# RWKV attention, tanh FFN and top-1 experts: logits and third block's first tile reordered, and one run of matmuls per tile from the fourth block on

## The chip, the cores and the metric

The kernel runs on one core of a Trainium2 chip. A core has a matrix engine (PE; its weight loads are shown apart as PEld), a vector engine (DVE), a scalar engine (ACT), a general engine (POOL) and an engine that here issues transfers (SP). The engines run side by side and wait for each other through semaphores. The metric is the device time of one execution in microseconds (us); lower is better.

## The reference

Four sequences of 768 tokens, eight heads of 48 numbers. Three stages follow each other:

```
for t in range(S):                                  # linear attention with a decaying state
    cur = einsum('bhd,bhe->bhde', u * k_t, v_t)
    y_t = einsum('bhd,bhde->bhe', r_t, state + cur)
    state = w * state + einsum('bhd,bhe->bhde', k_t, v_t)
h = x @ w_in; x = (h - tanh(h)) @ w_out             # 3072 tokens, 384 -> 2048 -> 384
expert_idx = argmax(normalize(x) @ normalize(expert_emb).T / tau)
out = gate * (relu(x @ w1[e]) @ w2[e])              # the one expert e that the token chose
```

Everything is float32.

## The kernel before, in words

The 3072 tokens are 24 tiles of 128, three tiles to a block, so eight blocks (0 to 7); a sequence is six tiles. The recurrence is done tile by tile: with the decay multiplied into r and k, the products of a tile's tokens among each other (*scores*, line 407) are masked and, with a diagonal for the bonus u, multiplied by v, and the state of the tile before is added (*values*, line 438); `state_product` (line 458) and `state_add` (469) carry the state on. The last tile of a sequence has no state product, the first no state part in values. On PE the three differ in shape: scores contract over 48 rows, the two head groups side by side; values write 32 columns each, four turns side by side; the state product writes 48 columns.

The FFN runs over a block of 384 tokens and over 16 slices of 128 of its 2048 inner columns. A *step* is one slice: `ffn1` (line 534, nine matmuls, for float32 is split into a high and a low part) into a PSUM bank ph, tanh and a split on ACT and DVE (lines 581 to 611), then `ffn2` (line 545, nine matmuls) into three banks acc that stay open over the block. ffn2 comes some steps after its ffn1. After its 16 steps a block is finished: normalized, logits by expert, choice, place counts (`finish`, PE lines 646 to 656). After all blocks the eight experts run over the tokens gathered by expert; that part is not touched.

The program is in three parts. A start, written out by hand for the attention of tiles 0 to 2 and the first slices. Then 22 hand-ordered steps: 6 of block 0 and the 16 of block 1, during which the FFN weights are converted into their parts (`convert_next`, `split`, DVE lines 253 to 259 and ACT line 266), and tiles 3 to 5 are done. The output weights also yield logits columns: class `Logits` has `turn` (transposes, line 282, and their copies wt, 284), `product` (291, lt 294) and `back` (298, 300), one per step in turn. Here the transposed k (`turned`, line 352) is copied to ktok by ACT (`turned_rows`, line 357), and the diagonal am is made by ACT in eight pieces (line 393). Then a loop over the blocks 0, 2, 3 ... 7: block j's steps, with the attention of the next block woven in by the generator `attention`, advanced by a counter, 18 pieces in 12 steps (8 for the rest of block 0). Each tile there is: decays, diagonal and ktok on DVE and POOL, scores, a few pieces later values and state product and results.

Within the engines' queues the instructions keep the order in which a scheduler puts them; it mostly follows the written order, may shift an instruction that it holds to be late, and is bound by `tc.issue_after`. PE takes its queue strictly in order. `fence` holds a tile's first instructions behind a given other one. `fill` (line 525) puts spare matmuls of ones into a bank that is written anew afterwards; NWARM (line 154) counts such matmuls at the very start.

Of the kernel before, what the change touches and what calls it, by code (L numbers as in the profile page):

```python
# [9 lines left out]
F32R = mybir.dt.float32r  # L10
# [3 lines left out]
AF = mybir.ActivationFunctionType  # L14
# [15 lines left out]
def rwkv__then__tanh_ffn__then__top1_moe_kernel(  # L30
# [14 lines left out]
    nc = tc.nc  # L45
# [32 lines left out]
    COL0 = (13, 15)  # L78
    NATT = 12
    NATT0 = 8  # L80
    ICOL = 6
    NWARM = 13
    ISTORE = 14
# [245 lines left out]
    class Att:  # L329
# [56 lines left out]

        def diagonal(self, on_act=False):
            self.am = []
            for g in range(2):
                a = work.tile([P, HP, P], F32, name="am", bufs=4)  # L390
                if on_act:
                    for q in range(HP):
                        nc.scalar.activation(out=a[:, q, :], in_=ident, func=AF.Copy, scale=self.cd[:, q, g:g + 1])
                else:
                    nc.gpsimd.tensor_tensor(out=a, in0=ident[:, None, :].to_broadcast([P, HP, P]),  # L395
                                            in1=self.cd[:, :, g:g + 1].to_broadcast([P, HP, P]), op=ALU.mult)
                self.am.append(a)
# [31 lines left out]
        def values(self, part=0, of=1, idle=0):  # L429
# [6 lines left out]
            for turn in self.todo[part * n // of:(part + 1) * n // of]:  # L436
                for g, (kk, lhs, rhs, start, stop) in enumerate(turn):
                    nc.tensor.matmul(out=self.py[32 * g:32 * g + 32, kk, :], lhsT=lhs, rhs=rhs, start=start, stop=stop)

# [38 lines left out]

    def attn_tile(n, xt):
        t = Att(n, xt)  # L480
        with ExitStack() as es:
# [13 lines left out]
        yield  # L495

        t.values()
        t.state()
# [15 lines left out]
    def attention(j):  # L514
        xts[j] = work.tile([P, NK, 2, TOK], F32R, name="xt")
        for n in range(TB * j, TB * j + TB):
            if 2 * TB + 1 < n + 1 < NTILE:
                load_rkv(n + 1)
            yield from attn_tile(n, xts[j])

# [665 lines left out]
    a[0].decay_k(nc.vector)  # L1186
    a[0].scores(range(HP), 5)
    a[0].turned()
# [63 lines left out]
    def attention_stage(i):  # L1252

        later = []
        for n, first in zip(range(TB, 2 * TB), START):
# [6 lines left out]
            if i == first + 1:  # L1262
# [3 lines left out]
                t.turned()  # L1266
                t.diagonal(DACT)
                t.turned_rows()
            elif i == first + 2:
# [22 lines left out]
    def step2(j, i, g):  # L1292
        if i == spans[j][0]:
            accs[j] = [ps.tile([P, DL], F32, tag="p", name=f"acc{t}") for t in range(TB)]
        ffn2(i, spans[j], g, wout, accs[j])

    steps = [(0, f) for f in range(FA)] + [(1, f) for f in range(NF)]
    spans[0] = (0, FA)
# [3 lines left out]
    for i in range(len(steps) + 1):  # L1302
# [33 lines left out]
        for f in later:  # L1336
            f()
        if i in turns:
            c = turns[i]
            logits.append(Logits(c, ready[2 * c + 1][0]))  # L1340
            logits[c].turn()
            done.add(2 * c + 1)
        if i - 2 in turns:
            logits[turns[i - 2]].back()
        if i - 1 in turns:
            logits[turns[i - 1]].product()
        if m < NF:
# [3 lines left out]
        if i == 9:  # L1351
            fence[2 * TB] = mark["glo"], last[1]
        load_next()
# [4 lines left out]
        if i == ISTORE:  # L1358
            store_x(1, xts[1])
    del xts[1]  # L1360

# [16 lines left out]
    for j in (0, *range(2, NB)):  # L1378
        xt = xts.pop(j)
        store_x(j, xt)  # L1380
        att = attention(max(j + 1, 2)) if j + 1 < NB else iter(())
        na = 0
        natt = NATT if j > 0 else NATT0
        for n, i in enumerate(range(*spans[j])):
            ph = ffn1([win(p, i) for p in range(2)], columns_of(xt), NK, TOK)
            pend.append((j, i, small_tanh(ph, squares(ph), j * NF + i)))
            while na < (n + 1) * 18 // natt:
                next(att, None)
                na += 1
            if len(pend) > LAG:  # L1390
                ffn2_next()
# [13 lines left out]
            if j == NB - 1 and i in COL0:  # L1405
                next(wides[0])
        for _ in att:
            pass
    while pend:
# [81 lines left out]
```

## Time and profile before

| | us |
|---|---|
| median of 3 runs | 800.43 (799.94 to 801.45) |
| profiled execution | 802.88 |
| its span, first to last instruction | 801.3 |
| PE busy | 772.8 (96%) |
| DVE busy | 506.8 (63%) |
| ACT busy | 451.5 (56%) |
| POOL busy | 283.9 (35%) |

The profile shows one execution. Its busy times are per engine, and its timeline lists instructions in order of time with neighbours of one kind merged; a row's duration is from the first start to the last end of the merged instructions. Since matmuls are pipelined, the distance from one row's start to the next row's start tells more than the durations. An idle time stands in brackets with what ended it.

### The profile page before, as it was taken

How to read it: one execution, taken by the hardware profiler on the slowest of the kernel's cores; microseconds unless marked ns; L12 is line 12 of the kernel's file. 1: busy time of each engine (PE TensorE's matmuls, PEld its weight loads, DVE VectorE, ACT ScalarE, POOL GpSimd, SP SyncE). 2: the span in 40 equal slices, each digit the busy share in tenths (PEclk: the TensorE clock that was granted, in tenths of full speed). 3: DMA queues.
4: the chain of work that ended last, by engine and by line, in shares of the span. 5: the costliest groups of instructions: out<-in, count | busy, mean ns of one | idle time of the engine just before them, and what ended most of it. 6: DMA issues, size and time to landing. Idle time of an engine off the chain costs nothing. (4 is left out here: it accounts for less than half of the span.)

```text
span 801.3 us, 15575 instructions
## 1 busy us (share of the span) xinstructions
PE 772.8 (96%) x5938; PEld 726.3 (91%) x5938; DVE 506.8 (63%) x1080; ACT 451.5 (56%) x1044; POOL 283.9 (35%) x296
## 2 busy tenths in 40 slices
PE   8889999999999999999999999999999999999992
PEld 5679898889999999999999999999989999999992
DVE  7977975677866865775875775766554445454410
ACT  5675776637456556556656666785443444444421
POOL 3721640383550740651651530143340412332111
PEclk9899999999999999999999999999999999999997
DMA  8834350233330240231222201160653534554300
GB/s 277 285 94 135 113 184 14 86 86 121 90 134 21 70 135 38 87 93 80 86 69 105 86 2 60 31 187 31 193 150 112 167 115 155 181 176 146 106 28 31
DMA packets 41861, 87.33 MB, mean 109 GB/s; under 512 B 9744, under 2 KB 21440, under 8 KB 40754
## 3 DMA queue, kind: packets, MB, share of 16 engines
q1 hardware_dynamic: 37042, 76.74, 29.8%
q0 software_dynamic: 4320, 9.51, 3.6%
q8 instruction: 48, 0.79, 0.4%
q14 instruction: 35, 0.29, 0.2%
q10 hardware_dynamic: 416, 0.00, 0.0%
HBM read 67.46 MB, written 19.47 MB: 108 GB/s over the span
## 5 line engine op out<-in xcount | busy, mean ns | idle before, releaser
L534 PE MATMUL ph<-xt,wq 128*128 128x384 f32 (+2 forms) x1712 | 341.3, 342 | 2.5 <-ACT wt L284 1.4
L534 PEld LDWEIGHTS ph<-xt,wq 128*128 128x128 f32 x1712 | 302.7, 189 | 7.6 <-ACT wt L284 1.5
L545 PE MATMUL acc<-wq,ghi 128*128 128x392 f32 (+2 forms) x1120 | 289.9, 344 | 0.0
L545 PEld LDWEIGHTS acc<-wq,ghi 128*128 128x128 f32 (+1 forms) x1120 | 200.3, 187 | 5.4 <-issue 1.4
L545 PE MATMUL acc<-wq,glo 128*128 128x392 f32 (+2 forms) x560 | 185.2, 341 | 0.3 <-DVE glo L611 0.3
L581 ACT ACTIVATE z<-ph 128x384 f32<-128x384 f32 x128 | 62.6, 489 | 88.9 <-PE ph L534 88.7
L545 PEld LDWEIGHTS acc<-wq,glo 128*128 128x128 f32 (+1 forms) x560 | 104.0, 187 | 1.3 <-DVE glo L611 0.6
L592 ACT ACTIVATE ghi<-ph 128x384 fp32r<-128x384 f32 x128 | 62.7, 490 | 73.6 <-DVE ph L591 69.0
L590 DVE TENSOR_TENSOR ph<-ph,z 128x384 f32<-128x384 f32 x128 | 71.9, 561 | 46.3 <-ACT z L581 45.4
L597 DVE TENSOR_TENSOR glo<-ph,ghi 128x384 fp32r<-128x384 f32 x128 | 70.9, 554 | 40.1 <-ACT ghi L592 39.7
L778 POOL DMA_INDIRECT out_dram<-ob,gts x27 | 28.8, 1068 | 155.4 <-ACT ob L858 149.9
L582 ACT ACTIVATE q<-z,sb_t 128x384 f32<-128x384 f32 x128 | 79.0, 617 | 3.6
L591 DVE SCALAR_TENSOR_TENSOR ph<-q,ph 128x384 f32<-128x384 f32 x128 | 71.8, 561 | 12.5 <-ACT q L582 3.6
L611 DVE SCALAR_TENSOR_TENSOR glo<-ph,ghi 128x384 fp32r<-128x384 f32 (+2 forms) x56 | 31.6, 564 | 74.9 <-ACT ghi L610 66.7
L594 ACT ACTIVATE mk<-z,lz_t 128x384 bf16<-128x384 f32 x128 | 77.1, 602 | 0.0
L610 ACT ACTIVATE ghi<-ph 128x384 fp32r<-128x384 f32 (+2 forms) x56 | 27.8, 497 | 72.5 <-PE ph L534 66.6
L827 DVE TENSOR_TENSOR wq<-eraw,wq 128x768 fp32r<-128x768 f32 x60 | 55.1, 956 | 12.0 <-ACT wq L826 10.4
L826 ACT ACTIVATE wq<-eraw 128x768 fp32r<-128x768 f32 x64 | 50.5, 838 | 6.5 <-DMA eraw<-in_moe_w_dram 6.1
L267 POOL TENSOR_TENSOR wq<-wraw,wq 128x768 fp32r<-128x768 f32 (+1 forms) x17 | 31.0, 1823 | 61.9 <-ACT wq L266 61.9
L380 POOL TENSOR_TENSOR rk<-rkv 128x384 f32<-128x384 f32 x18 | 18.4, 1024 | 92.2 <-ACT xr L631 45.2
L395 POOL TENSOR_TENSOR am<-ident,cd 128x512 f32<-128x512 f32 x36 | 37.4, 1064 | 10.2 <-DVE cd L385 10.2
L346 POOL TENSOR_TENSOR tt<-tt,tab_k 112x512 f32<-112x512 f32 x20 | 33.1, 1657 | 17.8 <-DMA tt<-in_cols_dram 17.8
(282 smaller groups left out, 888.0 us busy)
## 6 DMA issues: line engine op xcount, KB each, us to landing
eraw<-in_moe_w_dram SPq DMA_DIRECT2D x32, 768.0 KB, 5.1
rkv<-in_rows_dram SPq DMA_DIRECT2D x18, 640.0 KB
tt<-in_cols_dram SPq DMA_DIRECT2D x22, 448.0 KB, 4.0
xd<-xt SPq DMA_DIRECT2D x8, 1152.0 KB, 8.4
wraw<-in_moe_w_in_dram SPq DMA_DIRECT2D x8, 768.0 KB
wraw<-in_moe_w_out_dram SPq DMA_DIRECT2D x8, 768.0 KB, 6.9
xs<-xr SPq DMA_DIRECT2D x21, 192.0 KB, 2.2
rkv<-in_rows_dram SPq DMA_DIRECT2D x4, 256.0 KB, 10.7
```

Source lines behind the costliest of these rows:

```text
L395: nc.gpsimd.tensor_tensor(out=a, in0=ident[:, None, :].to_broadcast([P, HP, P]), in1=self.cd[:, :, g:g + 1].to_broadcast([P, HP, P]), op=A ...
L534: mark["ph"] = nc.tensor.matmul(out=ph, lhsT=lhs[a][:, kk, :], rhs=rhs(b, kk), start=(kk == 0 and p == 0), stop=(kk == nk - 1 and p == 2)).ins
L545: mm = nc.tensor.matmul(out=acc[t], lhsT=g[a][:, t * P:t * P + m], rhs=rhs(b, i), start=(i == span[0] and p == 0), stop=(i == span[1] - 1 ...
L581: nc.scalar.activation(out=z, in_=ph, func=AF.Square)
L582: nc.scalar.activation(out=q, in_=z, func=AF.Square, scale=SS, bias=sb_t)
L590: nc.vector.tensor_tensor(out=ph, in0=ph, in1=z, op=ALU.mult)
L591: nc.vector.scalar_tensor_tensor(out=ph, in0=q, scalar=KC, in1=ph, op0=ALU.add, op1=ALU.mult)
L592: mark["ghi"] = nc.scalar.activation(out=ghi, in_=ph, func=AF.Copy).ins
L594: nc.scalar.activation(out=mk, in_=z, func=AF.Relu, bias=lz_t, accum_out=zx[:, step:step + 1])
L597: mark["glo"] = nc.vector.tensor_tensor(out=glo, in0=ph, in1=ghi.bitcast(F32), op=ALU.subtract).ins
L826: nc.scalar.activation(out=hi[c][:, a], in_=t[:, a], func=AF.Copy)
L827: engs[s % len(engs)].tensor_tensor(out=lo[c][:, a], in0=t[:, a], in1=hi[c][:, a].bitcast(F32), op=ALU.subtract)
```

## The change

- Start: 17 instead of 13 first matmuls of ones, 4 instead of 5 fills in the first scores.
- Steps of blocks 0 and 1: ktok is issued behind the first half of the diagonal; in a step, Logits' back and product are now written ahead of turn. The decay of tile 7 gets the fence that tile 6 has.
- The third block's attention (`third`) begins in the last four of the 22 steps and is advanced by another rule in the rest of block 0.
- From block 2 on (attention of tiles 9 to 23), the generator is replaced by `prepare(n)` (decays, diagonal, ktok) and `turn(n)`: values and state product of tile n-1, scores of tile n right behind them, and only then the results, the state's sum and the mask. `turn` stands at steps 0, 4, 8, 12 of block 2 and 2, 7, 12 of the later ones.

```diff
@@ -76,10 +76,8 @@
     NEARLY = 1
     NNAR = 2
     COL0 = (13, 15)
-    NATT = 12
-    NATT0 = 8
     ICOL = 6
-    NWARM = 13
+    NWARM = 17
     ISTORE = 14
     FA = 6
     START = (0, 1, 2)
@@ -384,13 +382,17 @@
             self.cd = work.tile([P, HP, 2], F32, name="cd")
             nc.vector.tensor_reduce(out=self.cd.rearrange("p a b -> p (a b)"), in_=self.rk, op=ALU.add, axis=AX.X)
 
-        def diagonal(self, on_act=False):
+        def diagonal(self, on_act=False, between=None):
             self.am = []
             for g in range(2):
                 a = work.tile([P, HP, P], F32, name="am", bufs=4)
                 if on_act:
                     for q in range(HP):
-                        nc.scalar.activation(out=a[:, q, :], in_=ident, func=AF.Copy, scale=self.cd[:, q, g:g + 1])
+                        ins = nc.scalar.activation(out=a[:, q, :], in_=ident, func=AF.Copy,
+                                                   scale=self.cd[:, q, g:g + 1]).ins
+                    if between and g == 0:
+                        with tc.issue_after(ins):
+                            between()
                 else:
                     nc.gpsimd.tensor_tensor(out=a, in0=ident[:, None, :].to_broadcast([P, HP, P]),
                                             in1=self.cd[:, :, g:g + 1].to_broadcast([P, HP, P]), op=ALU.mult)
@@ -435,7 +437,8 @@
             n = len(self.todo)
             for turn in self.todo[part * n // of:(part + 1) * n // of]:
                 for g, (kk, lhs, rhs, start, stop) in enumerate(turn):
-                    nc.tensor.matmul(out=self.py[32 * g:32 * g + 32, kk, :], lhsT=lhs, rhs=rhs, start=start, stop=stop)
+                    mark["py"] = nc.tensor.matmul(out=self.py[32 * g:32 * g + 32, kk, :], lhsT=lhs, rhs=rhs,
+                                                  start=start, stop=stop).ins
 
         def result_hi(self):
             tok = slice((self.n % TB) * P, (self.n % TB + 1) * P)
@@ -476,8 +479,8 @@
             self.state_product()
             self.state_add()
 
-    def attn_tile(n, xt):
-        t = Att(n, xt)
+    def attn_tile(n):
+        t = Att(n, None)
         with ExitStack() as es:
             for x in fence.pop(n, ()):
                 es.enter_context(tc.issue_after(x))
@@ -494,6 +497,10 @@
         yield
         yield
 
+        j = n // TB
+        if j not in xts:
+            xts[j] = work.tile([P, NK, 2, TOK], F32R, name="xt")
+        t.xt = xts[j]
         t.values()
         t.state()
         t.result()
@@ -512,11 +519,42 @@
                               in_=xt.rearrange("p k i t -> p (k i t)").bitcast(F32))
 
     def attention(j):
-        xts[j] = work.tile([P, NK, 2, TOK], F32R, name="xt")
         for n in range(TB * j, TB * j + TB):
             if 2 * TB + 1 < n + 1 < NTILE:
                 load_rkv(n + 1)
-            yield from attn_tile(n, xts[j])
+            yield from attn_tile(n)
+
+    running = {}
+
+    def prepare(n):
+        t = running[n] = Att(n, None)
+        t.decay_r(nc.vector)
+        t.decay_k(nc.gpsimd)
+        t.bonus(nc.gpsimd)
+        t.sums()
+        t.diagonal()
+        t.decayed()
+
+    def turn(n):
+
+        t = running.pop(n - 1, None)
+        if t:
+            j = (n - 1) // TB
+            if j not in xts:
+                xts[j] = work.tile([P, NK, 2, TOK], F32R, name="xt")
+            t.xt = xts[j]
+            t.values()
+            t.state_product()
+        if n in running:
+            with tc.issue_after(mark["py"]) if t else ExitStack():
+                running[n].scores(range(HP))
+        if t:
+            t.result()
+            t.state_add()
+        if n in running:
+            running[n].causal()
+        if t and n + 1 < NTILE:
+            load_rkv(n + 1)
 
 
     def fill(bank, n):
@@ -1184,7 +1222,7 @@
     a[0].summed()
     a[0].decay_r(nc.vector)
     a[0].decay_k(nc.vector)
-    a[0].scores(range(HP), 5)
+    a[0].scores(range(HP), 4)
     a[0].turned()
     a[0].diagonal(True)
     routing_constants()
@@ -1264,8 +1302,7 @@
                 t.summed()
                 t.scores(range(HP))
                 t.turned()
-                t.diagonal(DACT)
-                t.turned_rows()
+                t.diagonal(DACT, t.turned_rows)
             elif i == first + 2:
                 t.causal()
             elif i == first + 3:
@@ -1294,6 +1331,7 @@
             accs[j] = [ps.tile([P, DL], F32, tag="p", name=f"acc{t}") for t in range(TB)]
         ffn2(i, spans[j], g, wout, accs[j])
 
+    third = attention(2)
     steps = [(0, f) for f in range(FA)] + [(1, f) for f in range(NF)]
     spans[0] = (0, FA)
 
@@ -1335,21 +1373,21 @@
             pass
         for f in later:
             f()
+        if i - 2 in turns:
+            logits[turns[i - 2]].back()
+        if i - 1 in turns:
+            logits[turns[i - 1]].product()
         if i in turns:
             c = turns[i]
             logits.append(Logits(c, ready[2 * c + 1][0]))
             logits[c].turn()
             done.add(2 * c + 1)
-        if i - 2 in turns:
-            logits[turns[i - 2]].back()
-        if i - 1 in turns:
-            logits[turns[i - 1]].product()
         if m < NF:
             last = split(*ready[m])
             if m % 2 == 0:
                 done.add(m)
         if i == 9:
-            fence[2 * TB] = mark["glo"], last[1]
+            fence[2 * TB] = fence[2 * TB + 1] = mark["glo"], last[1]
         load_next()
         if i == 1:
             behind.close()
@@ -1357,6 +1395,9 @@
             decay_rows()
         if i == ISTORE:
             store_x(1, xts[1])
+
+        if len(steps) - 4 <= i < len(steps):
+            next(third)
     del xts[1]
 
 
@@ -1378,15 +1419,22 @@
     for j in (0, *range(2, NB)):
         xt = xts.pop(j)
         store_x(j, xt)
-        att = attention(max(j + 1, 2)) if j + 1 < NB else iter(())
-        na = 0
-        natt = NATT if j > 0 else NATT0
+        na = 4
+
+        at = () if j in (0, NB - 1) else (0, 4, 8, 12) if j == 2 else (2, 7, 12)
+        n0 = TB * (j + 1) + (j > 2)
         for n, i in enumerate(range(*spans[j])):
             ph = ffn1([win(p, i) for p in range(2)], columns_of(xt), NK, TOK)
             pend.append((j, i, small_tanh(ph, squares(ph), j * NF + i)))
-            while na < (n + 1) * 18 // natt:
-                next(att, None)
+            while j == 0 and na < 5 + 3 * n // 2:
+                next(third, None)
                 na += 1
+            if n - 1 in at and n0 + at.index(n - 1) + 1 < NTILE:
+                prepare(n0 + at.index(n - 1) + 1)
+            if j == 2 and n == 0:
+                prepare(n0)
+            if n in at:
+                turn(n0 + at.index(n))
             if len(pend) > LAG:
                 ffn2_next()
             if n >= LAG:
@@ -1404,8 +1452,10 @@
                 next(ld, None)
             if j == NB - 1 and i in COL0:
                 next(wides[0])
-        for _ in att:
-            pass
+        if j == 0:
+            for _ in third:
+                pass
+            load_rkv(3 * TB + 1)
     while pend:
         ffn2_next()
     for _ in fin:
```

On PE, at the first of the later tiles (block 2's steps), the order of before. `pa` are scores, `py` values, `pst` the state product, `acc` and `ph` the FFN:

```order
L407 MATMUL pa_2707<-tt 128x128
L545 MATMUL acc_2596<-wq_77,ghi 128x392
...
L438 MATMUL py<-am,rkv_118 32x128 x4
L458 MATMUL pst<-rkv_118,ktok 48x48 x8
L545 MATMUL acc_2595<-wq_78,ghi 128x392
L545 MATMUL acc_2595<-wq_81,ghi 128x392
```

And the order now, at a tile of the same block:

```order
L440 MATMUL py<-am,rkv_123 32x128 x4
L461 MATMUL pst<-rkv_123,ktok 48x48 x8
L409 MATMUL pa_3075<-tt 128x128
L409 MATMUL pa_3076<-tt 128x128
...
L583 MATMUL acc_2567<-wq_79,ghi 128x392
L583 MATMUL acc_2567<-wq_82,ghi 128x392
```

The scores have moved from a place of their own between ffn1 and ffn2 to the place behind the state product of the tile before. The order has 14 such runs, one for each of the tiles 10 to 23.

On PE, in the third block's attention (tile 8, with the rest of block 0's steps), before:

```order
L407 MATMUL pa_2232<-tt 128x128 x4
L545 MATMUL acc_2033<-wq_82,ghi 128x392
...
L407 MATMUL pa_2233<-tt 128x128 x4
L545 MATMUL acc_2034<-wq_79,glo 128x392
...
L438 MATMUL py<-tt,st_120 32x128 x4
L545 MATMUL acc_2032<-wq_79,ghi 128x392
```

And now, the same tile:

```order
L409 MATMUL pa_2235<-tt 128x128
L409 MATMUL pa_2236<-tt 128x128
...
L583 MATMUL acc_2035<-wq_79,ghi 128x392
...
L440 MATMUL py<-tt,st_124 32x128 x4
L440 MATMUL py<-am,rkv_122 32x128 x4
```

Before, the scores of the two head groups are apart, and values begin, stop for FFN matmuls and go on. In the order now the scores, values and state products of tiles 7 and 8 stand whole, between ffn1 and ffn2; the scores of tile 6 have the first three matmuls of one group ahead of the first three of the other.

On PE, at the start of step 3, before and now (`pt` turn, `pl` product, `ps_k` transposes of k):

```order
L352 MATMUL ps_k<-ident,tt 128x112 x4
L282 MATMUL pt<-ident,wraw 128x128 x6
L291 MATMUL pl<-wt,ent 32x128 x6
L525 LDWEIGHTS ones_93
L525 MATMUL ph<-ones_93 128x384
```

```order
L350 MATMUL ps_k<-ident,tt 128x112 x4
L289 MATMUL pl<-wt,ent 32x128 x6
L280 MATMUL pt<-ident,wraw 128x128 x6
L563 LDWEIGHTS ones_93
L563 MATMUL ph<-ones_93 128x384
```

The product has moved ahead of the transposes; the four fills and the step's ffn1 stay behind both.

## Rows read from the trace of the kernel before

**Rows 1.** The page: busy time, share of the span, instructions.
```profile
PE 772.8 (96%) x5938; PEld 726.3 (91%) x5938; DVE 506.8 (63%) x1080; ACT 451.5 (56%) x1044; POOL 283.9 (35%) x296
```

**Rows 2.** Waits of PE: who waited for whom, total us, times, longest.
```profile
PE pl L291 <- ACT ktok L357: 2.4, 1, 2.4
...
PE ph L534 <- ACT wt L284: 1.4, 1, 1.4
...
PE py L438 <- DVE am L412: 0.9, 1, 0.9
```

**Rows 3.** Timeline of PE, block 2's steps: start us, us, line, count.
```profile
221.03 1.73 PE L534 MATMUL ph<-xt,wq 128*128 128x384 f32 x9
222.68 1.16 PE L407 MATMUL pa<-tt 48*128 48x128 f32 x16
223.77 0.63 PE L545 MATMUL acc<-wq,ghi 128*128 128x392 f32 x2
...
225.50 1.74 PE L534 MATMUL ph<-xt,wq 128*128 128x384 f32 x9
227.07 0.52 PE L545 MATMUL acc<-wq,ghi 128*128 128x392 f32 x2
...
228.68 1.74 PE L534 MATMUL ph<-xt,wq 128*128 128x384 f32 x9
230.35 0.42 PE L438 MATMUL py<-tt,st 112*32 112x128 f32 x8
...
232.03 0.56 PE L458 MATMUL pst<-rkv,ktok 128*48 128x48 f32 x16
232.52 0.63 PE L545 MATMUL acc<-wq,ghi 128*128 128x392 f32 x2
...
234.25 1.74 PE L534 MATMUL ph<-xt,wq 128*128 128x384 f32 x9
```

**Rows 4.** Busy time of each engine from tile 6's scores to tile 9's.
```profile
140.33:189.62 49.29, 48.05 (x463) 42.84 (x462) 33.30 (x75) 27.61 (x67) 29.89 (x28) 1.00 0.35 105
```

**Rows 5.** PE by line in that stretch: count, busy us, mean ns, idle.
```profile
L534 PE MATMUL ph<-xt,wq 128*128 128x384 f32 x100 | 19.8, 341 | 0.3 <-ACT xr L631 0.3
L545 PE MATMUL acc<-wq,ghi 128*128 128x392 f32 x60 | 16.5, 350 | 0.0
L545 PE MATMUL acc<-wq,glo 128*128 128x392 f32 x30 | 10.5, 348 | 0.0
```

**Rows 6.** Timeline of PE, tile 8's scores.
```profile
168.58 1.16 PE L407 MATMUL pa<-tt 48*128 48x128 f32 x8
169.67 0.45 PE L545 MATMUL acc<-wq,ghi 128*128 128x392 f32 x1
...
170.58 1.16 PE L407 MATMUL pa<-tt 48*128 48x128 f32 x8
```

**Rows 7.** Timeline of PE, start of step 3.
```profile
45.27 0.85 PE L291 MATMUL pl<-wt,ent 128*32 128x128 f32 x12 [2.41 <-ACT ktok L357]
...
46.58 3.24 PE L534 MATMUL ph<-xt,wq 128*128 128x384 f32 x9
```

**Rows 8.** Timelines of ACT and of DVE, the same time.
```profile
44.74 0.48 ACT L357 ACTIVATE ktok<-ps_k 128x384 f32<-128x384 f32 x1
...
38.97 1.18 DVE L343 TENSOR_TENSOR tt<-tt,tab_r 112x512 f32<-112x512 f32 x1
...
45.12 0.73 DVE L412 COPY_PREDICATED am<-cmask,pa 128x512 f32<-128x512 uint8 x1
```

**Rows 9.** A stretch of 10 us: busy time of PE, PEld, DVE, ACT, POOL, then PEclk.
```profile
40.00:50.00 10.00, 7.59 (x63) 6.36 (x66) 7.75 (x17) 6.82 (x20) 3.47 (x2) 0.83 0.30 91
```

**Rows 10.** Timeline of ACT, the wait of 1.4 us in rows 2.
```profile
87.15 0.88 ACT L266 ACTIVATE wq<-wraw 128x768 fp32r<-128x768 f32 x1
```

**Rows 11.** Timeline of PE, the first matmuls.
```profile
1.70 4.74 PE L154 MATMUL warm<-ones 128*128 128x512 bf16 x12
7.02 1.05 PE L370 MATMUL ps_cd<-u_pair,rows 112*128 112x2 f32 x8 [0.58 <-DVE rows L364]
```

## The prediction, made before the change was run

> **What bounds the kernel now.** I read the page's engine shares first, then PE's waits, then PE's timeline. The reader is to see that PE is busy for 772.8 of 801.3 us, 96% [rows 1], and that its named waits are few: 2.4, 1.4 and 0.9 us are the largest that the change touches [rows 2]. So neither another engine nor a transfer sets the time; PE's own queue does, and a change can only win in two ways: take one of these short waits away, or make PE do the same matmuls in less time. The second needs starts, not durations, since neighbouring matmuls overlap: how far one group's start lies from the next group's start. The row groups of block 2 give this for every kind of neighbour [rows 3].
>
> The profiled execution took 802.88 us, 2.45 more than the median of 800.43. The sum below is made against 802.88 and then carried over to the median.
>
> **One run of values, state product and scores: 14 times.** From block 2's steps [rows 3]: an undisturbed ffn1 takes 227.07 - 225.50 = 1.57 us to the start of ffn2, an undisturbed ffn2 228.68 - 227.07 = 1.61. With scores between, ffn1 takes 222.68 - 221.03 = 1.65 (0.08 more), the scores 223.77 - 222.68 = 1.09, and the ffn2 behind them 225.50 - 223.77 = 1.73 (0.12 more). A scores group thus costs 1.29. Values and state product cost 0.10 on the ffn1 ahead (230.35 - 228.68 = 1.67), 232.03 - 230.35 = 1.68 and 232.52 - 232.03 = 0.49 of their own, and 0.12 on the ffn2 behind (234.25 - 232.52 = 1.73): 2.39. Apart, the two cost 3.68. Put in one run, one way in and one way out of the FFN's matmuls goes: 0.10 + 1.68 + 0.49 + 1.09 + 0.12 = 3.48. So 0.20 per run, and for 14 runs 2.8 us. The number of matmuls stays the same, so nothing more can come from here.
>
> What the trace of before never shows is scores right behind a state product. Bounds: 0.20 per run, if that neighbour costs no more than an FFN matmul there; nothing, if going from one shape to the other costs as much again as the exit and the entry saved, so 0 to 2.8 in all. I take the upper end: the state product took its 0.49 to the FFN, and the nearest change from one small shape to another, values to state product, shows no gap beyond the rows' own time [rows 3].
>
> What could be late next: the run's four banks (two of scores, one each of values and state product) with the three open acc leave one of the eight for ph. By the waits that the programs write, the next ffn1's bank is one that the FFN's own DVE work gives back, which is done about a step ahead. I put no wait there; the rival below prices one. prepare's decays and diagonal on POOL and DVE come one step after the run before; the next run is four or five steps later (steps of 3.18 us, so some 13 us) and DVE and POOL were busy 33.30 and 29.89 of 49.29 us when attention ran beside the FFN [rows 4]: covered. The loads, SP's DMAs, are issued after the run of the tile before and have as long; they are not behind anything new.
>
> **The third block's attention.** From tile 6's scores to tile 9's took 49.29 us at the full clock [rows 4]. In it stand 190 FFN matmuls [rows 5], at 3.18 / 18 = 0.177 each 33.6 us; three tiles' scores whole, 3 x 1.29 = 3.9; three values with state product whole, 3 x 2.39 = 7.2. That is 44.7, and 4.6 us are over. I can name most of it: 0.9 and 0.3 are waits [rows 2, 5]; tile 8's scores ran as two groups, and each half took as long as a whole (169.67 - 168.58 = 1.09, the other alike by its length) [rows 6], which is 1.1 and another way in and out, 0.2: 1.3. The other 2.1 are values and state products cut in pieces, and finish's few counting matmuls. After the change the order has tiles 7 and 8 whole, each between ffn1 and ffn2. What stays: the counts, which I put at 0.3, and 0.5 for tile 6's scores, of which three matmuls per group still stand one group behind the other (half a split). So 4.6 - 0.8 = 3.8 us. Bounds: 2.2, if only the wait of 0.9 and the split scores go; 4.6.
>
> **The wait at 87 us.** PE waited 1.4 us for ACT's copy wt [rows 2], which stood behind the conversion wq of 0.88 [rows 10]. Now wt comes ahead of wq. The wq that gives way comes 0.9 later; POOL's difference and a later step's matmuls use it, and a step of 3.18 us ahead of that use covers it. The wait falls by about the row that stood in front, 0.8 of its 0.88; bounds 0 (something else is late in ACT's place) and 1.4.
>
> **The start.** PE stood 2.41 us before step 3's product, by the profile for ktok [rows 7], which ACT does behind eight diagonal pieces [rows 8]. In the order now the product is first and does not wait for ktok; the transposes behind it wait for DVE's first mask, the fills for ktok. The ktok still follows all eight pieces: the diagonal's new hook changes little here. What moves it is DVE: tile 7's decay (1.18) stood in its queue ahead of all this [rows 8] and is now held by the fence. The mask ended at 45.85 and so can end at about 44.7, ktok likewise at about 44.1. Half the transposes and the fills take an estimated 1.0, since product and fills took 46.58 - 45.27 = 1.31 [rows 7]. That lets ffn1 begin at 45.7 instead of 46.58: 0.9 us. Bounds: 0, if DVE fills the hole with another conversion, and 2.4, the whole wait.
>
> I cost the four more warming matmuls at 0. At 4.74 / 12 = 0.4 each they would take 1.6, of which the 0.58 that PE stood idle for DVE covers some [rows 11]; but the clock is slow only for the first of them, the fill left out gives time back, and the scores behind it waited for DVE in any case. The bounds are 0 and 0.5.
>
> Sum: 2.8 + 3.8 + 0.8 + 0.9 = 8.3. 802.88 - 8.3 = 794.6 for such an execution, and from the median 800.43 - 8.3 = 792.1 us.
>
> **A rule against the first term.** The trace shows the way between FFN and scores at 0.08 in and 0.12 out, and 0.10 in and 0.12 out for values [rows 3]. The Trainium skill (TensorEngine Tiling (Array Packing), section Key Properties) says that changing the tiling mode, not only the tile, drains the engine. Scores, values and the state product have different shapes, so by the rule the joint inside the run would be paid like any other; by the trace's sum it is free. This is the first rival, priced from rows.
>
> **Rivals.** (a) *The joint inside the run costs as much as a way in or out, 0.10*: then 14 x 0.10 = 1.4 come from the runs and the sum is 6.9, 793.5 us. For it: every change of shape shown here does cost 0.08 to 0.12. Against it: values to state product seems to cost nothing. Chance 0.22.
>
> (b) *The start's second clock dip goes too.* In 40 to 50 us the granted clock was 0.83 of full [rows 9], and the ffn1 after the wait took 3.24 us [rows 7] against 1.73 [rows 3]: the lower level of 1.2 GHz, half of 2.4. The wait stood right ahead of it. If a wait shorter by half leaves the clock full, 1.5 us more are won: 9.8, 790.6 us. Against it: some 1.5 us of idling remain. Chance 0.18.
>
> (c) *The waits in the third block and the start come back in another place*, so of 3.8 and 0.9 only 2.2 and 0 remain: 2.8 + 2.2 + 0.8 = 5.8, 794.6 us. Chance 0.12.
>
> (d) *Slower: the run starves ffn1 of a bank.* With seven banks taken, the ffn1 after the run waits until DVE gives one back. DVE owes after a run two masks (0.73 each [rows 8]), the state's sum and the low part of the result, which I estimate at the same, so 2.9; ffn2 covers 1.7 of it, and 1.2 per run remain. 14 x 1.2 = 16.8, so 800.43 - 8.3 + 16.8 = 808.9. It decides the sign from (8.3 + 1.6) / 14 = 0.7 per run on: with more the kernel is slower by over 0.2%. For it: the run does open the four banks at once, where before two had gone back. Against it: DVE is two thirds busy at most in such a stretch [rows 4], and the order gives ffn1 another bank. Chance 0.05.
>
> **How the numbers follow.** The forecast holds 0.43: 790.9 to 793.3 about 792.1. With (a), (b) and (c), 0.95 lie from 790 to 796. The extremes of all bounds together are 800.43 - (2.8 + 4.6 + 1.4 + 2.4 + 1.5) = 787.7 and 800.43 - 2.2 + 0.5 = 798.7; I take 788.5 to 796.5, which leaves (d) and a gain smaller than half out. About 0.2%, 1.6 us, is what a measurement of this kernel can tell from no change: 798.8 to 802.0 counts as the same. Faster 0.91; the same 0.05, from the corner where the bounds fall together or (d) costs half; slower 0.04, from (d).
>
> **What would show it.** In PE's timeline after: 14 runs of values, state product and scores with 3.3 us from the first start to the ffn2, and 1.7 for that ffn2; if the scores start 0.6 behind the state product, or take 1.2, (a) is right. Tiles 7 and 8's values at 1.68 and scores at 1.09 in one piece; no waits for am there. No wait of 1.4 before 90 us; one of about 1.1 to 1.5 at step 3, and the clock from 46 to 50 decides (b). A wait of PE for a mask, a state's sum or a result with some 14 cases would make the prediction wrong by (d).

## The result, and the profile after

The changed kernel took 806.75 us (median of 4 runs, 805.52 to 807.33) against 800.21 us: 1.0066 times the kernel before, 95% interval 1.0043 to 1.0090. Timed again later it was 1.0064 (1.0041 to 1.0086). It is slower by 0.66%, where 1% faster was forecast. The profiled execution took 805.52 us, span 803.7, so 2.6 us more than that of before.

PE's waits after, as in [rows 2] (who waited for whom, total, times, longest):

```profile
PE ph L572 <- DVE glo L635: 2.0, 1, 2.0
...
PE pa L409 <- issue: 1.6, 1, 1.6
...
PE pt L887 <- DMA ktab<-xs,gts: 1.2, 1, 1.2
PE pa L409 <- DVE glo L635: 1.1, 1, 1.1
...
PE pst L461 <- DVE se L732: 0.6, 1, 0.6
...
PE pt L280 <- DVE am L414: 0.6, 1, 0.6
...
PE ph L572 <- ACT wt L282: 0.3, 1, 0.3
```

The three waits that the change was costed on are down to 0.6, 0.3 and none. New are waits of scores (`pa`), state product (`pst`) and an ffn1 (`ph`). To place them I number the FFN matmuls of each trace (both have 3528) and compare when the same number starts, at points where the same attention is done:

| until FFN matmul | stretch | forecast, us | measured, us |
|---|---|---|---|
| 160 (88 us) | start and the wait at 87 us | -1.7 | -3.1 |
| 600 (190 us) | third block | -3.8 | -2.0 |
| 2100 (515 us) | runs, blocks 2 to 7 | -2.8 | +6.5 |
| 3528 (end) | experts | 0 | +1.0 |
| | sum | -8.3 | +2.4 |

The table sets one execution against one, so its sum is not the 6.5 us between the medians: the profiled execution of before took 2.7 us more than the median of its kernel, the one of after 1.2 us less. The first row depends most on the execution. With the same order of PE's matmuls up to there, matmul 160 began between 87.8 and 90.4 us in the fifteen traced executions with the changed start, and at 91.4 and 89.9 us in the two with the start of before (the second is e2 below).

The runs that nothing held up are as forecast. PE's timeline in block 3 (start, duration), to set beside [rows 3]:

```profile
300.47 0.56 PE L461 MATMUL pst<-rkv,ktok 128*48 128x48 f32 x16
300.96 1.16 PE L409 MATMUL pa<-tt 48*128 48x128 f32 x16
302.05 0.63 PE L583 MATMUL acc<-wq,ghi 128*128 128x392 f32 x2
...
303.78 1.75 PE L572 MATMUL ph<-xt,wq 128*128 128x384 f32 x9
```

State product to scores 0.49, scores 1.09, ffn2 behind them 1.73: the joint costs nothing. Ten of the 14 runs are like this (three of them, the last, have no state product). The price was paid in block 2, in the second run. PE there:

```profile
212.20 1.73 PE L572 MATMUL ph<-xt,wq 128*128 128x384 f32 x9
...
216.22 0.56 PE L461 MATMUL pst<-rkv,ktok 128*48 128x48 f32 x16 [0.61 <-DVE se L732]
218.37 0.46 PE L409 MATMUL pa<-tt 48*128 48x128 f32 x2 [1.59 <-issue]
219.98 2.07 PE L409 MATMUL pa<-tt 48*128 48x128 f32 x14 [1.15 <-DVE glo L635]
221.98 1.02 PE L583 MATMUL acc<-wq,ghi 128*128 128x392 f32 x2
...
225.08 2.44 PE L572 MATMUL ph<-xt,wq 128*128 128x384 f32 x9
```

Three waits, 3.35 us together, and behind them matmuls at nearly half the rate: from 219.8 to 226.6 us the granted clock was 0.5, the level of 1.2 GHz, which costs 3.4 us. In this stretch of 15 us (busy of PE, PEld, DVE, ACT, POOL, then the clock) its mean was 0.77:

```profile
215.00:230.00 15.00, 11.64 (x89) 10.90 (x79) 10.80 (x25) 6.75 (x16) 7.74 (x8) 0.77 0.24 76
```

The waits end with DVE's rows glo of the three newest FFN steps, which give back the banks that the run needs. The built program says the same: in the second run the state product waits for the glo of one step, the first half of the scores for the next one's, the second half for that of the ffn1 right ahead of the run. (The profile names other events for the first two waits, but each ends some 0.1 us behind the end of such a glo.) DVE was late with all three. Its timeline, with idle time in brackets:

```profile
203.97 0.56 DVE L449 TENSOR_TENSOR xt<-py,xt 128x384 fp32r<-128x384 f32 x1
209.77 0.69 DVE L341 TENSOR_TENSOR tt<-tt,tab_r 112x512 f32<-112x512 f32 x1 [5.25 <-DMA tt<-in_cols_dram]
210.38 1.36 DVE L414 COPY_PREDICATED am<-cmask,pa 128x512 f32<-128x512 uint8 x2
211.64 0.56 DVE L628 TENSOR_TENSOR ph<-ph,z 128x384 f32<-128x384 f32 x1
...
214.59 0.55 DVE L383 TENSOR_REDUCE cd<-rk 128x8 f32<-128x384 f32 x1 [1.72 <-POOL rk L379]
...
215.52 0.55 DVE L635 TENSOR_TENSOR glo<-ph,ghi 128x384 fp32r<-128x384 f32 x1
...
217.75 0.52 DVE L635 TENSOR_TENSOR glo<-ph,ghi 128x384 fp32r<-128x384 f32 x1
...
219.37 0.56 DVE L635 TENSOR_TENSOR glo<-ph,ghi 128x384 fp32r<-128x384 f32 x1 [0.56 <-ACT ghi L630]
```

For 5.25 us DVE's queue stood behind tile 11's decay, which waited for its load. The FFN's row of 211.64 had its input since 207.8. Then the queue stood for 1.72 us more behind tile 11's next row, cd, which needs a product of POOL's that was late by the same load. The load was issued at 202.94 and came right behind the last of finish's scatters to a DRAM table; POOL, which needs it too, began at 209.82. SP's timeline:

```profile
202.94 0.34 SPq L319 DMA_DIRECT2D tt<-in_cols_dram  x1
```

and POOL's:

```profile
201.08 0.95 POOL L715 DMA_INDIRECT tab<-tokid,irow  x1 [0.30 <-issue]
204.09 0.84 POOL L475 TENSOR_TENSOR st<-st,pw 112x384 f32<-112x384 f32 x1 [2.06 <-DVE st L470]
209.82 1.81 POOL L344 TENSOR_TENSOR tt<-tt,tab_k 112x512 f32<-112x512 f32 x1 [4.89 <-DMA tt<-in_cols_dram]
```

The first eight packets of that load took some 2.1 us each, most later ones 0.16. The other new wait, 2.0 us at 168 us, also comes from DVE: tile 9's decay, which the scheduler had drawn up into the third block, took 6.13 us instead of 0.69, while POOL worked without a pause until 167.48, from 162.48 on in five rows and with the scatter ahead of them. DVE, POOL and PE:

```profile
161.89 6.13 DVE L341 TENSOR_TENSOR tt<-tt,tab_r 112x512 f32<-112x512 f32 x1
167.95 0.55 DVE L628 TENSOR_TENSOR ph<-ph,z 128x384 f32<-128x384 f32 x1
```

```profile
162.48 0.85 POOL L475 TENSOR_TENSOR st<-st,pw 112x384 f32<-112x384 f32 x1
163.27 1.30 POOL L344 TENSOR_TENSOR tt<-tt,tab_k 112x512 f32<-112x512 f32 x1
...
166.47 1.01 POOL L379 TENSOR_TENSOR rk<-rk,u_bc 128x384 f32<-128x384 f32 x1
```

```profile
170.34 1.85 PE L572 MATMUL ph<-xt,wq 128*128 128x384 f32 x9 [2.01 <-DVE glo L635]
```

### The profile page after: what moved, and what is told of

It is laid out like the page before. It is cut to its first block, busy times and chain, and to the rows that moved or that the text cites. A ratio compares the mean times of both kernels' runs of the same rounds, so it can differ in the third digit from the quotient of the medians.

```text
span 803.7 us, 15611 instructions
## 1 busy us (share of the span) xinstructions
PE 772.8 (96%) x5941; PEld 731.0 (91%) x5941; DVE 495.8 (62%) x1080; ACT 449.0 (56%) x1044; POOL 283.8 (35%) x296
## 5 line engine op out<-in xcount | busy, mean ns | idle before, releaser
L619 ACT ACTIVATE z<-ph 128x384 f32<-128x384 f32 x128 | 62.4, 488 | 87.8 <-PE ph L572 87.6
L635 DVE TENSOR_TENSOR glo<-ph,ghi 128x384 fp32r<-128x384 f32 x128 | 70.9, 555 | 46.1 <-ACT ghi L630 44.7
L475 POOL TENSOR_TENSOR st<-st,pw 112x384 f32<-112x384 f32 x16 | 13.4, 837 | 104.2 <-DVE st L470 92.1
```

The lines of the kernel that those rows point to most:

```text
L619: nc.scalar.activation(out=z, in_=ph, func=AF.Square)
L635: mark["glo"] = nc.vector.tensor_tensor(out=glo, in0=ph, in1=ghi.bitcast(F32), op=ALU.subtract).ins
```

## The experiments

**Which part is slow.** Two kernels, the start and third block without the runs, and the runs alone on the kernel before. The diffs of this part show only the lines that matter.

```diff
 # e1: the changed kernel, blocks 2 to 7 as before
-            if n in at:
-                turn(n0 + at.index(n))
+            while j > 0 and na < (n + 1) * 18 // 12:
+                next(att, None)
 # e2: the kernel before, with prepare and turn from block 2 on
+            if n in at:
+                turn(n0 + at.index(n))
```

> The changed kernel with its start and its third block, but from block 2 on with the attention of the kernel before (no runs). Theory A (the loss sits in block 2, where tile 11's decay waits for its load at the head of DVE's queue and PE then waits for banks): PE has no waits at scores or state products of tiles 10 and 11 and no low clock in block 2; what start and third block gave, about 5 us with the wait of 2.0 us that they brought, remains: 795 us (793.5 to 797). Rival B (start or third block are slower than the trace makes them look): 802 us or more.

Measured: 0.9933 of the kernel before (0.9906 to 0.9959), 796.3 us. No waits in block 2 and full clock: theory A, not B. The edit takes away the runs and the late load together, so it does not tell which of the two it is.

> The kernel before with the runs of values, state product and scores from block 2 on as the only edit. Theory A: tile 11's load is again issued about when finish's scatter to the DRAM table ends and lands late, DVE is blocked, PE waits some 3.4 us and runs at the lower clock for some 7 us: about 800.2 + 7.5 - 2.8 = 805 us. Rival C (the runs themselves are good, the stall comes only from how start and third block have moved finish against the load): 797.4 us. Rival D (the joint inside a run costs): 798.8 us or more with no waits shown.

Measured: 1.0078 (1.0052 to 1.0103), 808.75 us. The same three waits (1.5, 1.6 and 1.15 us) and 6.8 us at half clock at 221 us, DVE and POOL again behind the load (POOL idle 5.2 us). So the loss belongs to the runs' part, and to A.

**First attempts to mend it.** One fence, and one decay moved:

```diff
 # e3, in block 2 for tile 11
-                prepare(n0 + at.index(n - 1) + 1)
+                with tc.issue_after(mark["glo"]) if j == 2 and n == 5 else ExitStack():
+                    prepare(n0 + at.index(n - 1) + 1)
 # e4, tile 8; e5, tile 9
-            t.decay_r(nc.vector)
+            t.decay_r(nc.gpsimd if n == 8 else nc.vector)
```

> The changed kernel with one edit: in block 2, tile 11's decays are held behind the DVE row glo of the step in which they are written, so that they no longer stand ahead of that step's FFN rows in DVE's queue while the load is on its way. Theory A: DVE's idle time of 5.2 us for the load goes or moves behind the FFN's rows; PE's waits of 0.6, 1.6 and 1.15 us in the second run go, and with them the 6.8 us at the lower clock: 806.7 - 3.4 - 3.4 = 800 us. Rival E (a run simply takes too many banks, whatever DVE does): the waits stay, 806 us or more.

Measured: 1.0022 (1.0003 to 1.0041). Half of the forecast gain: one wait of 2.2 us is left, and 3.4 us at half clock. DVE no longer waited for the load but stood 4.2 us for the next row of tile 11, cd, which needs POOL's product, late by the same load. PE's wait that is left ended, like those before, right behind a glo (216.90; the scores began at 216.99). The fence had moved the wait along the queue.

> The changed kernel with one edit: tile 8's decay of r is done by POOL instead of DVE. Theory F (that DVE row took 6.1 us instead of 0.7 since it reads two operands from SBUF, which DVE does not get to while POOL works through its own rows without a pause, and the FFN's rows stood behind it): no such row on DVE, PE's wait of 2.0 us for glo at 168 us goes: 804.7 us. Rival G (the DVE row was long because its input came late): the FFN's rows and PE's wait stay as they are or POOL's row is as late: 806.7 us.

Measured: 1.0004 (0.9986 to 1.0022), but the long DVE row was still there (5.2 us at 163.1): it is tile 9's. The profiled execution took 805.74 us like the changed kernel's; I draw nothing from this run.

**The second attempt**, with the changed kernel beside it:

> The changed kernel itself, timed beside the next three on the same chip. All theories: about 1.006 of the kernel before, as at first.

Measured: 1.0064 (1.0041 to 1.0086).

> The changed kernel with one edit: tile 9's decay of r (the DVE row that took 6.1 us at 161.9; the run before this had moved tile 8's by mistake) is done by POOL. Theory F (DVE could not get at its second SBUF operand while POOL worked without a pause): no row over 1 us on DVE there, PE's wait of 2.0 us for glo at 168 goes, 2 us less than the changed kernel. Rival G (the row was long because its input came late): the wait stays.

Measured: 1.0012 (0.9994 to 1.0029), some 4 us less than the changed kernel. The row is gone from DVE, POOL does it in 1.3 us and PE's wait at 168 us is gone (the ffn1 behind starts at once); POOL's timeline, then PE's:

```profile
163.17 1.30 POOL L341 TENSOR_TENSOR tt<-tt,tab_r 112x512 f32<-112x512 f32 x1
```

```profile
168.18 1.75 PE L572 MATMUL ph<-xt,wq 128*128 128x384 f32 x9
```

Rival G is out: POOL read the same load from 163.17 on, so the input was there. Theory F has PE's wait right, but not the DVE row: in its place another one stood until POOL's string of rows ended at 168.61. It takes 0.16 us in the trace after (at 170.75), and no wait of PE followed it:

```profile
164.58 4.07 DVE L733 TENSOR_SCALAR se<-se 128x3 f32<-128x3 f32 x1
```

The other 2 us I did not trace. Part of them can be the clock: in the trace of e9 the same wait was followed by 3.4 us at the lower clock (172.5 to 175.9), which is 1.7 us.

```diff
 # e7: load tile n+2's r and k in turn(n), in a third buffer
+            if n + 2 < NTILE:
+                load_tt(n + 2)
```

> The changed kernel with one edit: the decayed r and k of the tiles from 11 on have a third buffer (space that the weights' conversion has left), so each tile's load is issued one run earlier; tile 11's is thus on the chip long before finish's scatter. Theory A (the load, slow right behind the scatter, held DVE's queue, and PE's second run waited for the banks that DVE gives back late): DVE has no idle time of 5 us there, PE's waits of 0.6, 1.6 and 1.15 us go and with them the 6.8 us at the lower clock: 6.7 us less than the changed kernel. Rival E (a run takes more banks than DVE gives back in time anyway): the waits stay, less than 1 us of difference.

Measured: 1.0022 (1.0001 to 1.0042), and the waits in block 2 stayed (1.5, 1.5 and 1.2 us). That reads like a refutation; DVE's row shows that it is not:

```profile
208.30 0.69 DVE L353 TENSOR_TENSOR tt<-tt,tab_r 112x512 f32<-112x512 f32 x1 [5.75 <-DMA tt<-in_cols_dram]
```

Tile 11's decay had gone to 130 us, and the scheduler had put tile 12's into the same hole, which waited for tile 12's load, issued at the same moment behind the same scatter. The edit had changed the tile, not the place.

> Both edits together, the third buffer and tile 9's decay on POOL. By theories A and F 8.7 us less than the changed kernel, about 0.995 to 0.996 of the kernel before; by E and G no less than the changed kernel.

Measured: 1.0011 (1.0001 to 1.0022), with the waits in block 2 as in the run before. That is what e5 has alone; the third buffer added nothing to it, for the reason just told.

**Moving the scatter instead of the load.**

```diff
 # e10 (three steps); e14 one, e15 two
-            if n >= LAG:
+            if n >= (LAG + 3 if j == 2 else LAG):
                 next(fin, None)
```

> The changed kernel with one edit: in block 2 the pieces of block 0's finish come three steps later, so that its scatter to the DRAM table follows tile 11's load instead of going right ahead of it. (The third buffer had not put this to the test: the scheduler filled the hole in DVE's queue with tile 12's decay, which then waited for tile 12's load at the same place.) Theory A2 (the load is slow since it comes right behind the scatter; DVE's queue waits for it, whichever tile it is): the load lands in about 3.5 us instead of 6.6, DVE idles under 2 us there, PE's waits of 3.4 us in the second run shrink to under 1 and the clock stays full in block 2: 6 us less than the changed kernel, about 0.999 of the kernel before. Rival E (the run's banks are late anyway): the waits stay, no difference.

Measured: 0.9963 (0.9946 to 0.9981), about 8 us less than the changed kernel. The load, issued at 198.88, is used by POOL at 203.04, the second run's state product and scores have no wait, and the clock is full (SP, POOL and PE, and last the stretch as above: busy times and the clock):

```profile
198.88 0.34 SPq L319 DMA_DIRECT2D tt<-in_cols_dram  x1
```

```profile
203.04 1.82 POOL L344 TENSOR_TENSOR tt<-tt,tab_k 112x512 f32<-112x512 f32 x1 [1.30 <-DMA tt<-in_cols_dram]
```

```profile
216.57 0.56 PE L461 MATMUL pst<-rkv,ktok 128*48 128x48 f32 x16
217.07 1.16 PE L409 MATMUL pa<-tt 48*128 48x128 f32 x16
```

```profile
215.00:230.00 15.00, 14.53 (x119) 13.62 (x112) 7.80 (x18) 5.50 (x15) 7.45 (x8) 1.00 0.34 76
```

Rival E is out: the same runs take the same banks. PE's order changed in block 2 with this edit, the load's distance to the scatter with it; both belong to it.

> The edit before, and tile 9's decay of r on POOL. Theory A2 with F: 8 us less than the changed kernel, about 0.996 of the kernel before.

Measured: 0.9939 (0.9915 to 0.9962), 797.3 us. Now tile 12's load came right behind the scatter. It took 7.5 us from issue to use and DVE stood 5.1 us for it, but PE waited only 0.7 us there.

> The changed kernel with the decays of r of tiles 9 and 11 on POOL; PE's order is that of the changed kernel, the scatter and the load stay where they are. Theory A2 (what makes the load's lateness cost time is that a DVE row stands in front of the FFN's rows and waits for it): DVE has no idle time of 5 us, the FFN's rows are in time, PE's waits in the second run go or shrink to under 1.5 us although the load is as late as before: 5 to 8 us less than the changed kernel. Theory H (the late load itself holds PE's scores): PE's wait for tile 11's decay stays at 2 us or more.

Measured: 1.0019 (1.0005 to 1.0034). DVE's wait for the load was gone, and PE's three waits had become one, of 2.56 us from 215.7 on. It is not theory H: POOL's decays of tile 11 had ended at 211.89. The profile names POOL's am, which ended at 217.50; the built program has the first half of the scores wait for a glo of DVE, which ended at 218.19, 0.1 us ahead of them. DVE's queue had stood again, for 4.65 us, behind cd, as in e3 (POOL, DVE and PE):

```profile
210.55 1.34 POOL L344 TENSOR_TENSOR tt<-tt,tab_k 112x512 f32<-112x512 f32 x1
```

```profile
214.83 0.55 DVE L383 TENSOR_REDUCE cd<-rk 128x8 f32<-128x384 f32 x1 [4.65 <-POOL rk L379]
...
217.64 1.14 DVE L635 TENSOR_TENSOR glo<-ph,ghi 128x384 fp32r<-128x384 f32 x2
```

```profile
218.29 2.49 PE L409 MATMUL pa<-tt 48*128 48x128 f32 x16 [2.56 <-POOL am L397]
```

So the late load holds DVE's queue by two rows, the decay and cd; taking the one away leaves the other in front of the FFN's rows. In this execution 6.8 us ran at half clock. It is one of four that took 804.0 us or more at a mean granted clock of 0.980 to 0.982; the other eight took 801.5 to 803.0 at 0.985 or 0.986.

> All three edits: finish later in block 2, decays of r of tiles 9 and 11 on POOL. If A2 and F hold, 8 us less than the changed kernel; whether it also beats the kernel without runs, 0.993 of the kernel before, depends on the gain of 0.2 us per run, of which 2.8 us in all were forecast: then about 0.990 to 0.996.

Measured: 0.9951 (0.9929 to 0.9972): inside the range, and no better than e11.

**What the runs are worth when nothing holds them up.**

> The changed kernel with finish two steps later in block 2 and tile 9's decay of r on POOL. Three steps later (the run before) had tile 12's load come right behind the scatter instead of tile 11's: 7.5 us from its issue, DVE idle for 5.1, PE's waits there 0.7 us. Theory A2: with two steps the scatter lies between the two loads, both land in about 4 us, PE has no wait over 0.5 us in block 2's runs; with the runs' 2.8 us the kernel comes to about 0.990 of the kernel before. Theory J (the runs are worth nothing even undisturbed): no better than 0.993.

Measured: 0.9918 (0.9899 to 0.9937). The two loads took 4.0 and 4.6 us from issue to DVE's row, and the waits of PE that are named in block 2's runs are of 0.3 and 0.2 us, as theory A2 had it. The interval does not decide theory J.

> The same with one step. Theory A2: the scatter is still behind tile 11's load, so no large wait in block 2 either: 0.990 to 0.994.

Measured: 0.9931 (0.9913 to 0.9949), with no wait named in block 2's runs.

> Without the runs (the attention of the kernel before from block 2 on), start and third block as in the changed kernel, tile 9's decay of r on POOL. Its DVE row took 3.2 us without this edit, but no wait of PE followed: about 0.993 of the kernel before, by all theories. If the runs are worth their 2.8 us, the two other kernels of this call lie 2 to 3 us below it; by theory J they don't.

Measured: 0.9908 (0.9890 to 0.9926), 795.0 us against 803.0: the lowest of all these kernels, and it has no runs. The three intervals overlap, but the two kernels with runs do not lie 2 to 3 us below it, and by the medians (796.8 and 797.2) they lie above: theory J. In the traces, measured as in the table from FFN matmul 600 to 2100, e14 took 0.4 us less than the kernel before, e15 1.1 more and e16 the same. The gain of 2.8 us is in the joints and goes again inside the runs. From the starts of the groups: in e14 values, state products and scores of tiles 9 to 23 took 2.7 us longer in all than 1.68, 0.49 and 1.09 each, in e15 4.2; in e16 not one took longer. Two kinds: scores 0.1 to 1.1 us late in a few runs (by banks, as I take it), and values that meet finish's scatter, 1.0 us late in block 3 of e14 (PE's timeline, then POOL's):

```profile
269.68 0.43 PE L440 MATMUL py<-tt,st 112*32 112x128 f32 x8
...
271.85 0.27 PE L440 MATMUL py<-tt,st 112*32 112x128 f32 x1 [0.33 <-issue]
...
272.38 0.56 PE L461 MATMUL pst<-rkv,ktok 128*48 128x48 f32 x16
```

```profile
270.17 0.96 POOL L715 DMA_INDIRECT tab<-tokid,irow  x1 [0.30 <-issue]
```

No engine released PE at 271.85. A fetch of instructions of 16 KB ran just then, from 270.87 on, and took 2.6 us, where those around it took 1.0 to 1.4. That it held PE fits, but no run here took it away, and in the trace of the changed kernel a fetch of 3.3 us, from 404.4 on, fell into a run that lost nothing.

## Why the prediction was wrong

- **Start and the wait at 87 us**: right in direction and, for what the change did, near the forecast, as far as one execution shows. Step 3's ffn1 began at 46.11, 0.5 and not 0.9 us earlier, since the mask ended at about 45.0 instead of 44.7. The wait at 87 fell to 0.3, a gain of 1.1 for 0.8 forecast. Most of the rest, 1.4 us, is luck of the execution: the values behind that ffn1 came 1.8 us later instead of 3.2, at full clock as rival (b) has it, but (b)'s reason is not shown. The stretch at the lower clock ahead of it was longer by as much, 10.2 us (28.6 to 38.9) instead of 6.8, and in e2, with the start and the wait of before, ffn1 ran at full clock too (after, then e2):

```profile
45.05 0.62 PE L280 MATMUL pt<-ident,wraw 128*128 128x128 f32 x3 [0.56 <-DVE am L414]
...
46.11 1.87 PE L572 MATMUL ph<-xt,wq 128*128 128x384 f32 x9
47.91 1.08 PE L440 MATMUL py<-am,rkv 128*32 128x128 f32 x32
```

```profile
45.23 0.85 PE L291 MATMUL pl<-wt,ent 128*32 128x128 f32 x12 [2.29 <-ACT ktok L357]
...
46.53 1.87 PE L568 MATMUL ph<-xt,wq 128*128 128x384 f32 x9
```

- **Third block**: the term of 3.8 was right for what was counted: -2.0 measured is -4.0 with the wait of 2.0 at 168 us set aside, and -4.1 to -4.5 in the eight kernels with tile 9's decay of r on POOL. The wait was missed. It is not of the third block's attention at all, but of `prepare` for tile 9.
- **The 14 runs**: 0.20 in each of the ten that nothing held up, as worked out, and rival (a) is refuted: the joint is free. The trace bears out the sum and not the extra drain that I drew from the Trainium skill's rule on changes of mode (TensorEngine Tiling (Array Packing), section Key Properties).
- **The step that failed** is the paragraph behind that sum: "What could be late next ... I put no wait there", with "prepare's decays ... covered" and "the loads ... are not behind anything new". I had asked after the bank of the next ffn1, and not after the run's own three banks for state product and scores, which it takes from the three newest FFN steps, the last of them right ahead. Each is given back by DVE. And the load of the next tile, issued behind the run, was new behind something: finish's scatter. I had taken the margin of 13 us from run to run; the margin that counts is the one step from the load's issue to the first DVE row that waits for it, since the FFN's rows stand behind that row: 5.25 us in this case, and 1.72 more behind cd. With the scatter moved (e10) the event of the second run was gone.
- **Rival (d)**, slower by starved banks, named the right kind of place, with a price per run (1.2 us, 14 times) where it was one event of 6.8 us (3.35 of waits, 3.4 of clock) and some 2.5 us of small ones (state product at 201.6 1.1 late, values at 213.9 0.7, scores at 281 and 343 0.2 and 0.3). I gave it 0.05. The chances did not fit each other either: the forecast and (a) to (c) had 0.95, all of it faster, and faster got 0.91.
- **Left open**: 1.0 us more at the first experts, PE's wait for gathered tokens at 573 us. It is there in every kernel with runs that I looked at (1.1 to 1.6 us), 0.3 and 0.5 in the two without. And why e5 and e4 were timed lower than their profiled executions suggest. Part of it is the choice of execution: e4's, 805.74 us at a mean clock of 0.981, is the longest of twelve, of which the three shortest took 800.0 to 801.3 at 0.984; e5's took 803.03 at 0.982, and four took 800.5 to 801.4 at 0.984 to 0.987. What kept the clock up in those is not shown.

## What to carry to other kernels

A longer run of matmuls saves only its joints, 0.2 us here, and asks for all its banks, operands and instructions at one time: list every semaphore that it waits for, with who gives it back and what stands ahead of that in its queue. A load's margin ends at the first row that waits for it at the head of an in-order queue, not at the consumer that one has in mind. And when a mended kernel shows the same wait, look for whether a scheduler has put the next piece of the same kind into the same hole before calling the cause refuted.

## What the runs showed of the hardware

- Transfers right behind the scatter to DRAM were slow: tile 11's load took 6.9 us from issue to use instead of 4.2, tile 12's 7.5 in e11, where it had become the one behind the scatter. By distance: issued while the scatter still ran, tile loads took 8.1 to 8.3 us to their first row (e2, e3, e7); 0.8 to 0.9 us behind its last row, 6.7 to 7.5; 3.1 us behind, 4.6 (e15); 5.7 us behind, 3.6 (e14); ahead of it, 4.0 to 4.3. Fetches of instructions there took up to 2.8 and 3.5 us in the kernel before (at 166 us), unnoticed, since PE was in FFN matmuls then.
- DVE's row with both operands in SBUF took 6.13 us instead of 0.69 while POOL ran five rows without a pause, and ended 0.5 us after them. In e1 POOL's string had a gap of 0.05 us at 165.2, and there the row ended at 165.75, after 3.16 us. Rows that read one operand from PSUM did not stand: in e5 a glo took 0.56 us amid such a string, at 163.55. The Trainium skill (SBUF — State Buffer, section SBUF: two separate sides) says that such a DVE row and a POOL row lock each other out, whichever starts first, for the whole instruction. The trace agrees that DVE is locked out; it was for a string of five POOL rows, 5.0 us, and not for one. The row of 4.07 us in e5 reads one tile from SBUF and stood as well.
- The three waits in block 2, 3.35 us together, were followed by 6.8 us at the lower clock; e3's one wait of 2.2 by 3.4 us of it; e12's one of 2.56 by 6.8 us; the single wait of 2.0 us at 168 by none in this trace, but by 3.4 us in another execution of the same kernel (e9).
